# Attention with a relative bias and a gated MLP on one core: block transposes on VectorE, an eight-tile value product, and f16 operand pairs

## The chip, the cores and the metric

The kernel runs on one core of a Trainium2 chip. The core has a matmul engine (PE, whose weight loads the profile lists apart as PEld), three engines for everything else (VectorE or DVE, ScalarE or ACT, GpSimd or POOL), and SyncE (SP), whose queue issues most of the DMAs. Each engine works through its own instructions in order and waits on semaphores for the others. Matmul results land in PSUM, eight banks of 2 KB per partition; everything else is in SBUF. POOL is given no work on PSUM here. The metric is the device time of one execution in microseconds.

## The reference

Eight batches of eight heads, 576 positions, head size 64. The attention has a bias that a small two-layer network computes from the relative position, the same for all batches. Its output, with the heads side by side, is the input x of the gated MLP: a causal convolution of five taps per channel, a sigmoid of it as the gate, and two 512 x 512 products.

```python
scores = scale * np.matmul(q, k.transpose(0, 1, 3, 2))
x = (psi_rel / psi_i)[..., None]
h = np.maximum(x @ w1 + b1, 0.0)
bias = h @ w2
scores = scores + bias.transpose(2, 0, 1)[None, :, :, :]
scores = scores - np.max(scores, axis=-1, keepdims=True)
attn = np.exp(scores)
attn = attn / (np.sum(attn, axis=-1, keepdims=True) + 1e-09)
return np.matmul(attn, v).astype(np.float32)
...
for k in range(K):
    gate_pre += conv_w[k][None, None, :] * xp[:, k:k + S, :]
gate = 1.0 / (1.0 + np.exp(-gate_pre))
val = x @ w_val
return (gate * val @ w_out).astype(np.float32)
```

q, k, v and the bias network are f32; the convolution's weights and the two MLP matrices arrive as f64, which the kernel reads as pairs of 32-bit words and turns into a high and a low f32 part.

## The kernel before

**Planning.** The program does not issue its instructions in the order in which the code stands. `add` (line 87) records a task: the engines that may run it with a cost on each, the tasks it depends on, a priority, and the ring slots it takes and uses. `order` (line 100) then plays a greedy schedule through with these costs, and the tasks are emitted in its order. `OFFS` (line 56) shifts the priority of each kind of task, `LOAD` (line 55) weighs its cost when an engine is picked, `BUFS` (line 44) gives the slots of each ring, `LOOK` how far ahead of priority a task may take one, `PAIR_AT` and `MLP_AT` place each pair and each batch's MLP on the axis of priorities.

**Bias.** `bias_rows` (line 317) runs once for each 16 rows of positions: four relu passes on ACT, DVE or POOL (lines 338 and 340), matmuls with the second layer on four column tiles (line 359), an added constant on ACT or DVE (line 378), and a store of the skewed rows to DRAM. `load_bias` reads a chunk of 128 rows for a pair of heads back into SBUF when a run of pairs begins.

**Pairs.** `order` of line 275 lists 32 pairs of heads: `RUNS` (line 39) goes through the heads in two groups of four (two pairs, l = 0 and 1), in four runs; within a run the bias tiles stay. `pair` (line 526) has five chunks of query rows, four of 128 and one that holds the last 64 of both heads. For each: `qkm` multiplies Q and K in f32 on two row tiles, one head each (line 617, and line 629 for the last chunk); `logits` (line 659) adds the bias on DVE and takes the row extreme; `expo` (line 671) is the exponential on ACT with the row sum.

The attention weights must then be turned, keys onto partitions, and there are two ways, picked by `TRANS` (line 43). In 13 pairs POOL or DVE normalises (`norm`, line 716), PE transposes 128 x 128 blocks with the identity (line 756), and ACT or DVE copies them out of PSUM (`tev`). In the other 19 the exponentials are split into a high and a low f16 part (`top`, line 247 on ACT, and `rest`, line 254 on POOL), both are turned by a transposing DMA (`swap`, line 790), V is scaled and split in the same way (lines 559 to 586), and the division by the row sum comes after the value product: the reciprocals are transposed and spread over the partitions on PE (`rtp`, `rb`, lines 876 and 883) and multiplied in on DVE (`mu`, line 887). The value product itself (`piece`, line 826, and `rem_mm`, line 902) works on two column tiles of 64, one per head.

A pair of the batch's first run writes its x to DRAM (`store`), one of the second run puts it directly into the tile `xp`; the other half is read back (`ldx`).

**MLP.** `mlp` (line 943) runs for a batch when its four pairs are done. The convolution works on half rows of 288 in PSUM, on DVE (`taps`, line 1016); only the last batch uses `conv`, `prod` and `acc` on whole rows (lines 966 to 981). `val` (line 1073) and `outp` (line 1130) multiply high and low parts, three products for each, in the 32-bit single-pass format F32R; `split_hi`, `split_lo`, `ghi` and `glo` (lines 247 to 254) make those parts, `gf` (line 1083) multiplies the gate in, `ote` copies the result out of PSUM.

**PSUM.** The ring `sp` has two slots of two banks for QK, the ring `ps` four single banks for everything else.

## Time and profile before

| | |
|---|---|
| median of 3 runs | 762.93 us (762.93 to 766.36) |
| span of the profiled execution, first to last instruction | 759.0 us |
| granted clock of PE, mean | 0.995 |
| logits passes on DVE (line 659) | 256 of 750 ns and 32 of 820 ns |
| exponentials on ACT (line 671) | 256 of 774 ns and 32 of 826 ns |
| QK matmuls (line 617) | 1024 instructions of 64 rows x 128 columns, 288 moved |
| value product (line 826) | 1140 instructions in f16, 520 in f32 |
| HBM read and written | 61.03 and 25.05 MB |
| DMA packets | 263754, of which 231538 under 512 B |

An f32 matmul is two instructions in the list, an f16 or F32R one is one. "Busy" of a group is the time in which at least one of its instructions ran. Instructions of one engine overlap a little, so groups sum to more than the engine's busy time. The profiled execution ran 3.9 us shorter by its span than the median, which has what lies before the first and after the last instruction.

### The profile page before, as it was taken

To read this page: it belongs to the slowest core of one execution; us is meant where nothing else is said; L and a number is where in the kernel's file an instruction comes from. 1 tells how busy PE (TensorE), PEld (TensorE's weight loads), DVE (VectorE), ACT (ScalarE), POOL (GpSimd) and SP (SyncE) were. 2 spreads that over 40 slices of the span, in tenths; PEclk is the share of its full clock that TensorE was granted. 3 is DMA by queue.
4 is the path that set the end of the run, shared out by engine and by line. 5 is a ranking of instruction groups with operands and counts; after the bars stand their busy time and mean duration, and the time that the engine had idled before them with its cause. 6 is when DMAs were issued, how large, how long until landed. Compare 5 with 4: busy or idle time off the path is not lost.

```text
span 759.0 us, 17283 instructions
## 1 busy us (share of the span) xinstructions
PE 716.5 (94%) x6091; PEld 485.7 (64%) x6091; DVE 587.5 (77%) x1606; ACT 580.8 (77%) x1302; POOL 476.1 (63%) x550
## 2 busy tenths in 40 slices
PE   5577999999999999999899999999999999999997
PEld 2124666665566666767566677666767786767886
DVE  6996878777789897886759778869998878856830
ACT  6996788767578897889767876789797967797642
POOL 0002467765455685777975494859797587768852
PEclk9999999999999999999999999999999999999999
DMA  8898442968332878899999599599999999999702
GB/s 293 284 287 287 134 119 69 223 198 260 127 111 82 165 157 200 175 196 186 221 207 197 162 243 274 119 221 214 212 175 222 218 265 243 255 193 187 134 29 70
DMA packets 263754, 144.48 MB, mean 190 GB/s; under 512 B 231538, under 2 KB 231796, under 8 KB 263668
## 3 DMA queue, kind: packets, MB, share of 16 engines
q1 hardware_dynamic: 258420, 133.95, 76.7%
q10 hardware_dynamic: 5248, 9.44, 3.9%
q8 instruction: 48, 0.79, 0.4%
q14 instruction: 38, 0.31, 0.1%
HBM read 61.03 MB, written 25.05 MB: 113 GB/s over the span
## 4 chain that ended last, share of the span: by engine, by line
PE 50%; POOL 3%; DMA 3%; DVE 3%; ACT 2%; issue 1%; SPq 0%; POOLq 0%; DVEq 0%; ACTq 0%
PE t_ps L1073 12%; PE t_ps L1130 11%; PE t_sp L617 10%; PE t_ps L826 9%; DMA t_pt<-t_d 3%; PE t_sp L629 2%; PE t_ps L883 2%; PE t_ps L756 2%; POOL t_d L254 2%; PE t_ps L902 2%; PE t_ps L876 1%; DVE t_d L659 1%; ACT t_d L671 1%; DVE xl L254 0%; POOL xl L254 0%
## 5 line engine op out<-in xcount | busy, mean ns | idle before, releaser
L671 ACT ACTIVATE t_d<-t_d,nm 128x576 f32<-128x576 f32 x256 | 197.9, 774 | 67.7 <-DVE nm L659 67.0
L254 POOL TENSOR_TENSOR t_d<-t_d 128x576 f16<-128x576 f32 x152 | 198.1, 1315 | 36.1 <-ACT t_d L247 29.5
L659 DVE CUSTOM_DVE_ANT_0 t_d<-t_sp,bias 128x576 f32<-128x576 f32 x256 | 187.7, 750 | 35.6 <-PE t_sp L617 24.7
L716 POOL TENSOR_SCALAR t_d<-t_d,rinv 128x576 f32<-128x576 f32 x104 | 79.6, 777 | 148.5 <-DVE rinv L698 91.7
L617 PE MATMUL t_sp<-t_qk 64*128 64x288 f32 x1024 | 169.3, 432 | 3.2 <-DVE nm L659 3.1
L826 PE MATMUL t_ps<-t_pt,t_w 128*64 128x256 f16 (+1 forms) x1660 | 140.9, 311 | 4.8 <-DMA t_pt<-t_d 2.5
L617 PEld LDWEIGHTS t_sp<-t_qk 64*128 64x128 f32 x1024 | 95.0, 188 | 52.9 <-issue 13.4
L1016 DVE SCALAR_TENSOR_TENSOR t_ps<-t_xp,convw,t_ps 128x288 f32<-128x288 f32 x168 | 87.2, 519 | 5.6 <-ACT t_ps L1007 2.7
L1073 PE MATMUL t_ps<-xh,wv 128*128 128x320 f32 (+1 forms) x512 | 84.4, 302 | 1.1 <-DVE rt L249 1.1
L1073 PEld LDWEIGHTS t_ps<-xh,wv 128*128 128x128 f32 x512 | 71.9, 188 | 12.4 <-issue 7.3
L247 ACT CAST t_d<-t_d 128x576 f16<-128x576 f32 x113 | 74.6, 668 | 2.9 <-PE t_ps L756 0.4
L1130 PE MATMUL t_ps<-wo,gh 128*128 128x512 f32 x256 | 71.9, 409 | 0.7 <-ACT gh L247 0.6
L826 PEld LDWEIGHTS <-t_w 128*64 128x64 f16 x1140 | 57.4, 109 | 22.2 <-issue 18.9
L756 PE MATMUL t_ps<-identr,t_d 128*128 128x128 f32 x468 | 67.1, 281 | 0.8 <-POOL t_d L716 0.3
L756 PEld LDWEIGHTS t_ps<-identr,t_d 128*128 128x128 f32 x468 | 50.8, 140 | 23.0 <-issue 9.8
L247 ACT COPY t_pt<-t_ps 128x512 f32<-128x512 f32 (+1 forms) x104 | 50.8, 514 | 13.8 <-PE t_ps L756 13.7
L1130 PEld LDWEIGHTS t_ps<-wo,gh 128*128 128x128 f32 x256 | 44.7, 188 | 18.3 <-issue 6.4
L247 ACT COPY t_w<-t_ps 128x512 f32<-128x512 f32 (+2 forms) x65 | 32.6, 501 | 31.2 <-PE t_ps L1130 20.2
L1083 DVE TENSOR_TENSOR t_w<-t_ps,t_w 128x256 f32<-128x256 f32 (+1 forms) x64 | 29.0, 454 | 33.0 <-PE t_ps L1073 26.6
L254 POOL TENSOR_TENSOR gl<-t_w,gh 128x256 fp32r<-128x256 f32 x53 | 40.8, 771 | 16.2 <-PE t_ps L1130 12.8
L826 PEld LDWEIGHTS t_ps<-t_pt,t_w 128*64 128x64 f32 x520 | 33.0, 136 | 28.0 <-issue 10.7
L251 POOL TENSOR_SCALAR t_d<-t_d 128x576 f16<-128x576 f32 x36 | 25.2, 700 | 37.9 <-ACT t_d L671 30.4
(116 smaller groups left out, 1207.4 us busy)
## 6 DMA issues: line engine op xcount, KB each, us to landing
t_qk<-qkd SPq DMA_DIRECT2D x32, 608.0 KB, 4.7
bias<-bias_d SPq DMA_DIRECT2D x32, 576.0 KB, 5.1
bias_d<-t_be SPq DMA_DIRECT2D x36, 295.5 KB, 4.7
out<-t_w ACTq DMA_DIRECT2D x32, 256.0 KB, 3.2
t_w<-vd SPq DMA_DIRECT2D x19, 320.0 KB, 3.5
xs<-t_w SPq DMA_DIRECT2D x16, 288.0 KB, 3.6
t_xp<-xs SPq DMA_DIRECT2D x8, 576.0 KB, 4.7
t_w<-vn SPq DMA_DIRECT2D x13, 320.0 KB, 5.1
```

What stands on the lines that cost most here:

```text
L247: A.copy(out=out, in_=in_)
L254: (V if e == "V" else G).tensor_tensor(out=out, in0=in0, in1=in1, op=ALU.subtract)
L617: T.matmul(ts[a][:, j, 0:hw], lhsT=q_[r, c * P : (c + 1) * P], rhs=k_[r, a * REM + j * hw : a * REM + (j + 1) * hw], start=True, stop=True,)
L659: V.tensor_tensor_reduce(out=part().rearrange("p (j f) -> p j f", j=2), in0=sp.t[:, :, 0 : w // 2], in1=bias.rearrange("p (j f) -> p j f", ...
L671: A.activation(out=part(), in_=part(), func=AF.Exp, bias=nms[c][:, a : a + 1], scale=-1.0, accum_out=sums[c][:, a, 0:1],)
L716: (G if e == "G" else V).tensor_scalar(out=t, in0=t, scalar1=rinvs[c][:, a : a + 1], scalar2=1.0, op0=ALU.mult, op1=ALU.mult,)
L756: T.transpose(t[:, k * P : (k + 1) * P], es[c].t[:, (k0 + k) * P : (k0 + k + 1) * P], ident)
L826: T.matmul(po.t[r, 0:256], lhsT=vt.t[:, v0 + t, r], rhs=pt[:, w, :, :] if tr else pt[:, :, w, :], start=(k == 0), stop=(k == 5 * len(prods ...
L1016: V.scalar_tensor_tensor(out=o, in0=x, scalar=cw, in1=t, op0=ALU.mult, op1=ALU.add)
L1073: T.matmul(pm.t[:, 0:w], lhsT=pools["wv"][wi][:, k, d * P : (d + 1) * P], rhs=xb.t[xi][:, k, 0:w], start=(q == 0 and k == 0), stop=(q == 2 ...
L1083: V.tensor_tensor(out=gf_.t[:, 0:w], in0=pm.t[:, 0:w], in1=gates[d].t[:, t0 : t0 + w], op=ALU.mult)
L1130: T.matmul(pm.t, lhsT=gb.t[gi][:, k, o : o + P] if o < 256 else gx.t[gi][:, k, :], rhs=pools["wo"][wi][:, k, :], start=(q == 0 and k == 0) ...
```

## The change

- The runs become nine short ones, `(0, (0,)), (1, (0, 1)), (0, (1, 2)), ...`: a batch's second half follows its first at once. The spill of x to DRAM is gone; each pair's x goes directly into `xp`. The bias tiles are loaded anew for each run.
- Both ways of turning the weights are replaced by one. POOL normalises every row (`norm`, POOL alone), DVE transposes blocks of 32 x 32 in f32 (`turn_`), and the value product runs in f32 on eight tiles at a time, 32 rows x 64 columns each: V is loaded four times over the partitions for it. PE transposes, transposing DMAs, the splits of weights and V, and the rescaling afterwards are gone.
- The last 64 queries of l = 0 and l = 1 are multiplied together on four tiles of 64 x 64 (`qkr`).
- The MLP's operands become pairs of f16 values. For this x, the weights and the result are scaled by powers of two that come from maxima: of V per batch (`scales`: a read of V, a reduction on DVE, a matmul with ones), of the weights once (`wm_red`, `wm_fin`). The scaling sits in the evictions (`ev`, `ote`), in `gf` and in the convolution's weights (`vm_cw`).
- The convolution of every batch is that of the last batch before, with the first of four channel blocks on DVE alone, and the sums of the other three on POOL alone.
- The ring `sp` has three slots instead of two and also holds the value product's output; `ps` has two banks instead of four. `OFFS`, `LOAD`, `LOOK`, `PAIR_AT` and `MLP_AT` have new numbers, and some costs in the tasks too; the planner's cost of a change of matmul mode is now given by mode.

```diff
-RUNS = ((0, (0, 1, 2, 3)), (1, (0, 4, 1, 5, 2, 6, 3)), (0, (4, 5, 6, 7)), (1, (7,)))
+RUNS = ((0, (0,)), (1, (0, 1)), (0, (1, 2)), (1, (2, 3)), (0, (3, 4)), (1, (4, 5)), (0, (5, 6)), (1, (6, 7)), (0, (7,)))
...
-BUFS = dict(w=13, d=5, pt=2, sp=2, ps=4, qk=3, rel=4, be=6, xp=2, xh=1, gh=1, gx=1, rt=2)
+BUFS = dict(w=10, d=5, pt=2, vx=2, sp=3, ps=2, qk=2, rel=3, be=6, xp=2, xh=1, gh=1, gx=1)
...
-DRAIN = 0.07
+DRAIN = (0.18, 0.21, 0.16, 0.16, 0.16)
...
-LOAD = dict(P=0.95, V=1.2, A=0.36, G=0.47, S=0.08)
+LOAD = dict(P=0.87, V=0.69, A=0.25, G=0.68, S=1.63)
...
+        def vm_red(e):
+            t = vb.t.rearrange("p j d -> p (j d)")
+            V.tensor_reduce(out=osc[b][:, 1:2], in_=t, op=ALU.max, axis=AX.X, apply_absolute_value=True)
...
+        nr = [add([("G", 0.73)], partial(norm, a=a), [t], h + heads + 0.6 + a / 2) for a in range(heads)]
...
+                def qkr(e, sps=sps):
+                    ts = [new(sp, [P, 2, 512], F32) for sp in sps]
+                    for j in range(2):
+                        for y, q_ in enumerate((qk, qk2)):
+                            for a, r in enumerate((top_, bot)):
+                                x = (j + a) % 2
+                                T.matmul(
+                                    ts[y][(top_, bot)[(a + y) % 2], x, 0:HS],
+                                    lhsT=q_.t[r, NM * P : S],
+                                    rhs=q_.t[r, S + x * HS : S + (x + 1) * HS],
+                                    start=True,
+                                    stop=True,
+                                )
...
+            def turn_(e, c=c, eb=eb, first=first):
+                if first is None:
+                    new(xt, [P, 2 * NM + 1, S], F32)
+                if c < NM:
+                    V.transpose(out=xt.t[:, c : 9 - c : 8 - 2 * c, :], in_=eb.t.rearrange("p (a f) -> p a f", a=2))
                 else:
+                    V.transpose(out=xt.t[:, NM, :], in_=eb.t)
...
+        avs = [Buf("sp") for _ in range(2)]
+
+        def av(e, j0):
+            if j0 == 0:
+                for sp in avs:
+                    new(sp, [P, 2, 512], F32)
+            pv = xt.t.rearrange("p s (j q) -> p s j q", q=32)
+            for j in range(j0, j0 + NJ // 3):
+                for i in range(4):
+                    for a in range(2):
+                        k = NM + (i // 2 == (a + l) % 2)
+                        r, o = slice(32 * i, 32 * i + 32), (top_, bot)[a]
+                        T.matmul(
+                            avs[i // 2].t[o, i % 2, 0 : 32 * k],
+                            lhsT=vx.t[r, j, o],
+                            rhs=pv[r, 0:k, j, :] if a == 0 else pv[r, 8 : 8 - k : -1, j, :],
+                            start=j == 0,
+                            stop=j == NJ - 1,
                         )
...
+            t = add([("A", 0.58), ("V", 0.5)], partial(ev, h=h), d, s0 + 13.5, [xo] if new_ else (), [avs[h]])
...
-                elif k >= 2:
-                    y = add([("A", 0.67), ("G", 0.75)], prod, d[:1], x - 0.2, [tmp], [xp])
-                    convs[k] = add([("V", 0.67), ("G", 1.3)], acc, [convs[k], y], x, (), [tmp])
+                elif k >= 1:
+                    y = add([("A", 0.67), ("G", 0.75)], prod, d[:2], x - 0.2, [tmp], [xp])
+                    convs[k] = add([("G", 1.45)], acc, [convs[k], y], x, (), [tmp])
                 else:
                     convs[k] = add([("V", 0.73)], conv, d, x, (), [xp])
...
-                        xb.t = [pools["mp"].tile([P, NK, 320], F32R, name=x, tag=x) for x in ("xh", "xl")]
+                        xb.t = [pools["mp"].tile([P, NK, 320], F16, name=x, tag=x) for x in ("xh", "xl")]
```

## The prediction

> **What bounds the kernel now.** I read the page's busy times first, then the busy time by stretch, the chain that ended last, and the groups by line.

> ```profile
> span 759.0 us, 17283 instructions
> PE 716.5 (94%) x6091; PEld 485.7 (64%) x6091; DVE 587.5 (77%) x1606; ACT 580.8 (77%) x1302; POOL 476.1 (63%) x550
> ...
> PE 50%; POOL 3%; DMA 3%; DVE 3%; ACT 2%; issue 1%; SPq 0%; POOLq 0%; DVEq 0%; ACTq 0%
> ```
> ```profile
> 0.00:80.00 80.00, 54.47 (x486) 22.75 (x487) 64.32 (x171) 62.82 (x135) 8.83 (x34) 0.96 0.84 278
> 80.00:720.00 640.00, 628.12 (x5396) 434.56 (x5393) 515.36 (x1421) 505.60 (x1141) 451.86 (x497) 1.00 0.85 188
> 720.00:759.10 39.10, 33.95 (x213) 28.39 (x212) 7.86 (x15) 12.37 (x27) 15.40 (x21) 0.99 0.14 48
> ```

> The columns of the second fence are the stretch, then PE, PEld, DVE, ACT, POOL busy, the granted clock, DMA share and GB/s. From 80 to 720 us, where the pairs run, PE is busy 628.1 of 640 us at full clock: it loses 1.9% and sets the pace. DVE and ACT stand idle a fifth of that stretch. The first 80 us (the bias rows) are not PE's: all three engines are below 81% there, and the pairs need those rows. The last 39 us are PE's again, the last batch's MLP, with DVE idle 31 of them. So the question is what PE still has to do, and which engine takes its place.

> **What PE loses.** The matmul groups, then pieces of the chain (start, length, line, instructions), which show a group's length from its start to the next group's:

> ```profile
> L617 PE MATMUL t_sp<-t_qk 64*128 64x288 f32 x1024 | 169.3, 432 | 3.2 <-DVE nm L659 3.1
> L826 PE MATMUL t_ps<-t_pt,t_w 128*64 128x256 f16 (+1 forms) x1660 | 140.9, 311 | 4.8 <-DMA t_pt<-t_d 2.5 <-ACT t_pt L247 1.7 <-ACT xh L247 0.6
> L756 PE MATMUL t_ps<-identr,t_d 128*128 128x128 f32 x468 | 67.1, 281 | 0.8 <-POOL t_d L716 0.3 <-ACT t_pt L247 0.2
> L629 PE MATMUL t_sp<-t_qk 64*64 64x320 f32 x256 | 41.4, 442 | 4.7 <-DVE nm L659 4.6
> L883 PE MATMUL t_ps<-rt,sel 2*128 2x256 f32 x76 | 26.4, 426 | 0.3 <-ACT t_w L855 0.3
> L902 PE MATMUL t_ps<-t_w 128*64 128x64 f16 (+1 forms) x830 | 23.0, 207 | 0.0
> L876 PE MATMUL t_ps<-identr,rinvs 128*2 128x128 f32 x76 | 14.3, 271 | 0.0
> L756 PE MATMUL t_ps<-identr,t_w 128*128 128x128 f32 x65 | 10.0, 279 | 0.7 <-POOL t_w L716 0.3 <-ACT t_pt L247 0.2
> L912 PE MATMUL t_ps<-identr,rinvs 128*64 128x64 f32 x76 | 5.9, 236 | 0.0
> ```
> ```profile
> 290.09 1.17 PE t_sp L617 x8
> ...
> 293.89 1.76 PE t_ps L826 x30
> ```
> ```profile
> 306.20 2.31 PE t_ps L826 x20
> ```
> ```profile
> 726.29 5.66 PE t_ps L1073 x48
> ```

> Value product, PE transposes and row rescaling (L826, L756 twice, L883, L902, L876, L912) make 287.6 us. The 17 PE groups of that view (nine stand here) sum to 785 where the page has 716.5, since neighbours overlap, so I scale by 0.91: 262 us go. What comes is, per pair, 18 steps of eight tiles, each an f32 product of two instructions, half of them 160 columns wide. L826's 20 f32 instructions are ten pairs on two column tiles in 2.31 us: 0.231 us for 256 columns, so 0.144 for 160. If all eight tiles run side by side the wider ones set the step: 18 x 2 x 0.144 = 5.2 us, and 0.2 for a group's start (L617: 1.17 us, of which four pairs of 288 columns at 256-column speed less its start, 0.24 each, are 0.96). 32 x 5.4 = 173 us. The trace has two row tiles side by side (L617) and two column tiles (L826), never four rows: bounds 4.3 us (18 steps of the mean 144 columns without any start) and 10.4 (four tiles at a time). I take 5.4, nearest to rows in which every tile shown does run beside its neighbour.

> The last queries, 41.4 us for 32 groups, become 16 groups of four tiles, 1.3 us each: 21, so 20 go. The MLP's f16 pairs: 30 f16 instructions of 256 columns on two column tiles take 1.76 us, 0.117 a pair; 48 single-pass f32 ones take 5.66, 0.118 each. Between nothing and the 8% that a group's start may hide, 0 to 16 us; I take 10. PE: 716.5 - 262 + 173 - 20 - 10 = **598 us**. It stops being the bound.

> **What DVE takes on.**

> ```profile
> L659 DVE CUSTOM_DVE_ANT_0 t_d<-t_sp,bias 128x576 f32<-128x576 f32 x256 | 187.7, 750 | 35.6 <-PE t_sp L617 24.7 <-DMA bias<-bias_d 3.8 <-POOL t_d L254 3.4
> L1016 DVE SCALAR_TENSOR_TENSOR t_ps<-t_xp,convw,t_ps 128x288 f32<-128x288 f32 x168 | 87.2, 519 | 5.6 <-ACT t_ps L1007 2.7
> L1016 DVE SCALAR_TENSOR_TENSOR t_w<-t_xp,convw,t_ps 128x288 f32<-128x288 f32 x56 | 28.8, 515 | 2.3
> L575 DVE SCALAR_TENSOR_TENSOR t_w<-t_w,vsc 128x640 f16<-128x640 f32 x19 | 20.7, 1090 | 0.5 <-ACT t_w L572 0.5
> L559 DVE TENSOR_REDUCE vsc<-t_w 128x1 f32<-128x640 f32 x19 | 15.4, 810 | 2.5 <-DMA t_w<-vd 2.5
> L249 DVE COPY t_pt<-t_ps 128x512 f32<-128x512 f32 x22 | 15.0, 682 | 0.2
> L966 DVE SCALAR_TENSOR_TENSOR t_w<-t_xp,convw,t_w 128x576 f32<-128x576 f32 x8 | 11.3, 1444 | 1.7 <-ACT t_w L970 1.7
> L887 DVE TENSOR_TENSOR t_xp<-t_xp,t_ps 128x256 f32<-128x256 f32 x24 | 10.0, 418 | 4.8 <-ACT t_xp L855 4.7
> L340 DVE TENSOR_SCALAR rel<-gt,sct,nb 128x576 f32<-128x576 f32 x6 | 3.1, 569 | 0.0
> ```
> ```profile
> 405.07 0.74 DVE L659 CUSTOM_DVE_ANT_0 t_d<-t_sp,bias 128x576 f32<-128x576 f32 x1
> 405.74 0.08 DVE L659 DVE_READ_ACCUMULATOR2_ANT nm<- 128x1 f32 x1
> 405.74 0.22 DVE L923 TENSOR_TENSOR t_xp<-t_xp,t_ps 128x64 f32<-128x64 f32 x1
> ```

> The timeline shows 0.67 us from one 0.74 us logits pass to the next instruction: packed, an instruction costs its length less 0.07, and 576 elements cost 0.60 + 0.07. A block transpose is on no row. Per pair there are four of 1,152 elements and one of 576. At the logits' 1.04 ns an element they cost 1.27 and 0.67 us, 5.75 a pair, **184 us** in all. Below stands the L340 speed (569 ns for 576, so 0.86 ns an element: 1.0 us), above the contended L966 (1444 ns: 2.9 us). I take the first, from passes that, like it, read one SBUF stream. [...]

> Removed: the convolution on half rows (L1016, 116.0), the value splits (L575, 20.7; L559, 15.4), the copies out of PSUM (L249, 15.0 and smaller), the rescaling (L887 and smaller), L966 (11.3): about 210 us, some 185 packed. Added besides the transposes: the first block's four taps, 576 wide with two SBUF inputs, which is L966's form: 32 x 1.44 = 46 (half of it if POOL were not in the way); the per-batch maximum over 2,304 elements (2.5 us by L559's speed) and the weights' maxima, 34 with their small steps; 38 more sums and reciprocals of the softmax, 6. Net 587.5 - 185 + 184 + 46 + 34 + 6 = 673. That base holds about 35 us which a full queue saves (some 500 of 1606 instructions that ran with nothing behind them, 0.07 each), and the greedy plan can send a few splits elsewhere: about **630 us**, bounds 605 and 670.

> **ACT and POOL.**

> ```profile
> L671 ACT ACTIVATE t_d<-t_d,nm 128x576 f32<-128x576 f32 x256 | 197.9, 774 | 67.7 <-DVE nm L659 67.0
> L254 POOL TENSOR_TENSOR t_d<-t_d 128x576 f16<-128x576 f32 x152 | 198.1, 1315 | 36.1 <-ACT t_d L247 29.5
> L716 POOL TENSOR_SCALAR t_d<-t_d,rinv 128x576 f32<-128x576 f32 x104 | 79.6, 777 | 148.5 <-DVE rinv L698 91.7
> L247 ACT CAST t_d<-t_d 128x576 f16<-128x576 f32 x113 | 74.6, 668 | 2.9 <-PE t_ps L756 0.4
> L981 POOL TENSOR_TENSOR t_w<-t_w 128x576 f32<-128x576 f32 x8 | 12.3, 1541 | 1.4 <-ACT t_w L976 0.9
> L247 ACT COPY t_pt<-t_ps 128x512 f32<-128x512 f32 (+1 forms) x104 | 50.8, 514 | 13.8 <-PE t_ps L756 13.7
> ```

> ACT drops casts and copies (74.6 + 50.8 and smaller) and takes products and evictions of about the same sum: it stays below 580. POOL drops the subtractions (198.1), and gets all 288 normalisations (0.777: 224) and 96 accumulations (1.541: 148): about 510. Neither binds; both are links between DVE's logits and its transposes. New waits: a transpose stands in DVE's queue until POOL has normalised both heads, and behind it stand the next logits, for which ACT waits; that is in the 3% below. The added loads I cost at nothing. By their shapes, 40 more main bias tiles of 0.59 MB, V four times over (1.18 MB a pair) and the maxima's reads are some 65 MB; at the 278 GB/s of the first 80 us that is 234 us of some 650, while 114 transposing DMAs and the spill of x go. The loads run under the previous pair's softmax; if that cover is gone, a late bias tile stops SP and the V and QK loads queued behind it, 5 us or so at each of eight changes of run.

> **The sum**, on the span of 759.0. DVE's 630; its idle in the first 80 us, 16 (80 - 64.3); its idle beside the last MLP, 28 (31 now); and between them 3% of some 560 us, 18, against the 1.9% that PE loses now, since DVE's work hangs on three engines. 630 + 16 + 28 + 18 = 692. The median, 762.9, lies 3.9 above the span, so **696 us**.

> **Rivals.**
> - *DVE packed like PE today, or less work* (splits elsewhere, taps uncontended): 605 to 615 + 44 + 6: 655 to 670.
> - *The PSUM ring is the clock.* There are three two-bank slots; a QK group takes two, and the value product's outputs hold two. Per pair, 4.5 times (1.17 + a 0.67 logits pass + 0.3 of hand-overs) is 9.6, and 5.4 of product with 1.5 of eviction and hand-over 6.9: 16.5 us at least, with no QK in those 6.9. DVE needs (692 - 80 - 39)/31 = 18.5 a pair. The 24.7 us for which logits wait on L617 speak for it, at two slots. So 0.45 us of queueing per group makes it equal to DVE; with 0.65 it is 19.4 a pair: 80 + 31 x 19.4 + 39 + 4 = 724; with 0.9, 20.5 and 759.
> - *Row tiles overlap poorly.* [...] Worked from rows: L617's 0.96 of 1.17 is 0.82; the product becomes 6.5 us, PE 633, and if half of the added 35 us falls where DVE waits for it, 714.
> - *Slower: the transpose takes two cycles an element*, 2.5 us. DVE rises by 128 x 1.2 + 32 x 0.6 = 173, to a time of 870. It turns from faster to slower at 1.27 + 67/144 = 1.74 us, since 144 full ones share the 67 us gained. L340 and L659 speak against it, L966's 2.9 for it.
> - *The eight tiles run four at a time*, 10.4 us: PE 758, time about 800, slower too.
> - *No gain:* the work removed from PE was all hidden. PE's 98% in the middle speaks against it.

> **Chances.** Forecast (672 to 725) 0.48; better packed 0.16; ring above 725, 0.16; poor row overlap 0.08; slower by transpose 0.06, by tiles 0.03; no gain 0.03. Eight in ten lie between 650 and 752: below it little of the packed case, above it the slower ones and the worst of the ring. Faster by over 0.5% (about what a measurement can tell here) 0.88, within 0.5% 0.03, slower 0.09.

> **What would show it.** Right: DVE busy above 88%, transposes near 1.3 us, the product in three groups of about 1.8 us, PE near 600 and below 90%, a chain split over engines. Wrong: transposes over 1.74 us; product groups over 2.2; logits waiting for L617's successor over 60 us in all with DVE below 85% (the ring); a granted clock under 0.98.

## The result: slower by 5.8%, and the profile after

The changed kernel takes 808.88 us (median of 4 runs, 806.53 to 813.1) where the kernel before takes 763.04: a ratio of 1.058, 95% interval 1.053 to 1.063. The forecast was 696, with 650 to 752 as its range, so the sign was wrong too. The first lines of the page of the changed kernel, its instruction queue, and its chain by engine:

```profile
span 804.7 us, 28607 instructions
...
PE 670.2 (83%) x12072; PEld 421.2 (52%) x12072; DVE 643.0 (80%) x1562; ACT 523.5 (65%) x1141; POOL 462.5 (57%) x548
...
q8 instruction: 95, 1.56, 0.8%
...
PE 26%; DVE 7%; issue 4%; POOL 1%; ACT 1%; DMA 1%; POOLq 0%; ACTq 0%; DVEq 0%
```

DVE, ACT and POOL are near or below what was forecast (630, below 580, about 510). PE fell by 46 us, not 118. Nothing is full: 83% is the largest share. Two things are new. PE has 12,072 matmuls and as many weight loads, twice as many as before (6,091 of each). And in the chain "issue", time in which an engine waits for nothing that the profile shows, went from 1% to 4%.

The groups of instructions by line give the place. The columns are those of before: line, engine, operation, tiles, shape, count, busy time, mean ns, and the idle time before them with what ended it.

```profile
L752 PE MATMUL t_sp<-t_qk 64*128 64x288 f32 x1024 | 203.0, 465 | 37.8 <-DVE nm L686 36.7 <-ACT xp L251 0.8
L811 PE MATMUL t_sp<-t_pt,t_vx 32*64 32x160 f32 (+1 forms) x9216 | 197.8, 308 | 60.7 <-issue 56.2 <-DVE nm L686 2.2 <-DVE xp L253 2.2
...
L772 PE MATMUL t_sp<-t_qk 64*64 64x288 f32 x256 | 22.9, 451 | 1.2 <-DVE nm L686 1.2
```
```profile
L686 DVE CUSTOM_DVE_ANT_0 t_d<-t_sp,bias 128x576 f32<-128x576 f32 x256 | 187.5, 739 | 23.8 <-PE t_sp L752 23.4
L790 DVE STREAM_TRANSPOSE t_pt<-t_d 128x1152 f32<-128x1152 f32 x128 | 173.3, 1362 | 29.4 <-PE t_sp L811 24.8 <-POOL t_d L712 4.3
...
L792 DVE STREAM_TRANSPOSE t_pt<-t_w 128x576 f32<-128x576 f32 x32 | 24.4, 763 | 0.6 <-POOL t_w L712 0.6
L626 DVE TENSOR_REDUCE osc<-t_vx 128x1 f32<-128x2304 f32 x8 | 20.3, 2539 | 1.4 <-DMA t_vx<-vf 1.4
```

L811 is the value product, and 56.2 us of "issue" stand before its instructions. The transposes cost what was forecast (1.36 us each and 0.76), but wait 24.8 us for the product. One product in the timeline (start, length, line, instructions, and in brackets the idle time before):

```profile
299.32 2.93 PE L811 MATMUL t_sp<-t_pt,t_vx 32*64 32x160 f32 x148
...
302.74 2.16 PEld L811 LDWEIGHTS t_sp<-t_pt,t_vx 32*64 32x64 f32 x128 [0.79 <-issue]
302.75 2.44 PE L811 MATMUL t_sp<-t_pt,t_vx 32*64 32x160 f32 x128 [0.50 <-issue]
306.75 0.22 PEld L811 LDWEIGHTS t_sp<-t_pt,t_vx 32*64 32x64 f32 x12 [1.84 <-issue]
306.75 0.52 PE L811 MATMUL t_sp<-t_pt,t_vx 32*64 32x160 f32 x12 [1.57 <-issue]
...
307.28 1.03 ACT L251 ACTIVATE xp<-t_sp,xsc 128x256 f32<-128x256 f32 x3 [6.49 <-PE t_sp L811]
...
307.45 1.38 DVE L790 STREAM_TRANSPOSE t_pt<-t_d 128x1152 f32<-128x1152 f32 x1 [6.84 <-PE t_sp L811]
```

The product breaks off twice, after 148 matmuls and after 128 more, and waits for nothing that is named. Between the two breaks lie 128 matmuls and 128 loads: 256 instructions. It is so in the whole trace. Inside products, 46 pauses are longer than 0.4 us, 71 us in all. If PE's instructions are numbered in the order of their starts, its semaphore instructions among them, 39 of these pauses (64 us) end with an instruction whose number leaves one and the same remainder when divided by 256; the other seven make 6 us. Queue q8, which carries instructions, moved 1.56 MB in 95 packets, 16 KB each, and 24,144 matmuls and loads are 94.3 times 256: one packet for each 256 of them. In the trace's DMA records the next packet starts 1.15 us (the median) after such a number is passed, and at 85 of the 95 such numbers not before: at these it is fetched once the packet before it is begun. The packets that the 39 pauses wait for take 0.9 to 1.4 us, and each pause ends 1.2 to 1.6 us after its packet has landed. Together that is some 3.5 us for 256 instructions. While PE pauses, ACT cannot empty the product's banks (6.49 us) and DVE cannot write the next transposed tile, since there are two of them (6.84 us).

The stretches show what is left. Columns: PE, PEld, DVE, ACT and POOL busy, the granted clock, DMA share, GB/s.

```profile
0.00:80.00 80.00, 55.50 (x398) 18.77 (x398) 64.21 (x177) 66.86 (x128) 10.74 (x29) 0.98 0.92 314
80.00:160.00 80.00, 52.86 (x998) 34.43 (x998) 67.31 (x158) 39.90 (x91) 42.72 (x44) 0.79 0.54 170
160.00:240.00 80.00, 63.36 (x1180) 43.52 (x1186) 74.40 (x171) 55.94 (x116) 60.82 (x58) 0.74 0.55 188
...
740.00:810.00 70.00, 56.77 (x856) 35.63 (x848) 37.39 (x92) 31.76 (x71) 23.34 (x25) 0.98 0.10 36
```

By the forecast's own sum: DVE works 643 us (forecast 630); it is idle 15.8 us in the first 80 (forecast 16) and 27.3 after 740 (64.7 - 37.4; forecast 28). What is left, 804.7 - 643.0 - 15.8 - 27.3 = 118.6 us, is its idle time in between, where the forecast had 18. Of the 113 us of the miss 101 lie there, and 13 in DVE's own work.

### The profile page after: what moved, and what is told of

Read it like the earlier page. It is cut to its first block, busy times and chain, and to the rows that moved or that the text cites. A ratio compares the mean times of both kernels' runs of the same rounds, so it can differ in the third digit from the quotient of the medians.

```text
span 804.7 us, 28607 instructions
## 1 busy us (share of the span) xinstructions
PE 670.2 (83%) x12072; PEld 421.2 (52%) x12072; DVE 643.0 (80%) x1562; ACT 523.5 (65%) x1141; POOL 462.5 (57%) x548
## 3 DMA queue, kind: packets, MB, share of 16 engines
q8 instruction: 95, 1.56, 0.8%
## 5 line engine op out<-in xcount | busy, mean ns | idle before, releaser
L712 POOL TENSOR_SCALAR t_d<-t_d,rinv 128x576 f32<-128x576 f32 x256 | 201.2, 799 | 128.1 <-DVE rinv L708 112.0
L811 PE MATMUL t_sp<-t_pt,t_vx 32*64 32x160 f32 (+1 forms) x9216 | 197.8, 308 | 60.7 <-issue 56.2
L752 PE MATMUL t_sp<-t_qk 64*128 64x288 f32 x1024 | 203.0, 465 | 37.8 <-DVE nm L686 36.7
L811 PEld LDWEIGHTS t_sp<-t_pt,t_vx 32*64 32x64 f32 x9216 | 173.3, 138 | 86.8 <-issue 75.5
L686 DVE CUSTOM_DVE_ANT_0 t_d<-t_sp,bias 128x576 f32<-128x576 f32 x256 | 187.5, 739 | 23.8 <-PE t_sp L752 23.4
L790 DVE STREAM_TRANSPOSE t_pt<-t_d 128x1152 f32<-128x1152 f32 x128 | 173.3, 1362 | 29.4 <-PE t_sp L811 24.8
L884 POOL TENSOR_TENSOR t_w<-t_w 128x576 f32<-128x576 f32 x96 | 137.2, 1430 | 22.3 <-ACT t_w L879 18.8
L944 PEld LDWEIGHTS <-wv 128*128 128x128 f16 x768 | 71.6, 100 | 49.1 <-issue 30.0
L944 PE MATMUL t_ps<-xh,wv 128*128 128x320 f16 (+1 forms) x512 | 80.1, 295 | 5.6 <-DVE t_w L954 3.7
L1006 PE MATMUL t_ps<-wo,gh 128*128 128x512 f16 x256 | 64.4, 384 | 1.0 <-ACT gh L243 0.4
L350 PE MATMUL t_sp<-rel,w 128*32 128x288 f32 (+17 forms) x352 | 48.0, 511 | 18.3 <-ACT rel L328 6.6
L879 ACT ACTIVATE t_w<-xp,convb 128x576 f32<-128x576 f32 x76 | 55.9, 763 | 4.4 <-DVE rinv L708 2.4
L350 PEld LDWEIGHTS t_sp<-rel,w 128*32 128x32 f32 x352 | 14.4, 116 | 50.8 <-ACT rel L328 18.5
```

The lines of the kernel that those rows point to most:

```text
L350: T.matmul(pb.t[32 * g : 32 * g + 32, j, 0 : y - x], lhsT=w28, rhs=rel[g].t[:, x:y], start=True, stop=True, tile_position=(0, 32 * g),)
L686: V.tensor_tensor_reduce(out=eb.t[:, a * S : (a + 1) * S].rearrange("p (j f) -> p j f", j=2), in0=sps[a].t[:, :, 0:HS], in1=bias.rearrange ...
L712: (G if e == "G" else V).tensor_scalar(out=t, in0=t, scalar1=st["r"][:, a : a + 1], scalar2=1.0, op0=ALU.mult, op1=ALU.mult)
L752: T.matmul(ts[a][:, j, 0:HS], lhsT=qk.t[r, c * P : (c + 1) * P], rhs=qk.t[r, S + j * HS : S + (j + 1) * HS], start=True, stop=True,)
L790: V.transpose(out=xt.t[:, c : 9 - c : 8 - 2 * c, :], in_=eb.t.rearrange("p (a f) -> p a f", a=2))
L811: T.matmul(avs[i // 2].t[o, i % 2, 0 : 32 * k], lhsT=vx.t[r, j, o], rhs=pv[r, 0:k, j, :] if a == 0 else pv[r, 8 : 8 - k : -1, j, :], start ...
```

## The experiments

Theory 1: PE's instructions arrive in packets of 256, one takes about 3.5 us from the start of the packet before it to its own use, and a product of 576 instructions (288 matmuls, 288 loads) waits for them. Theory 2: the tiles overlap worse than thought, so columns set its length. Theory 3: the order of work or the other engines set the time, and PE's pauses are cover.

**Fewer columns, same instructions** (after the first of the 18 steps a matmul moves 32 columns; most of the product is left out).

```diff
-                        k = NM + (i // 2 == (a + l) % 2)
+                        k = NM + (i // 2 == (a + l) % 2) if j == 0 else 1
```

> The changed kernel, but from the second of the 18 steps of the value product on, each matmul moves 32 columns instead of 128 or 160; it leaves out most of the product and issues as many instructions as before. Theory 1 (PE waits for its instructions: 256 of them per fetch, one fetch about every 3.5 us, so 576 instructions take 7.9 us whatever they compute): a product stays at 7 to 8 us and the time at 790 to 815 us. Theory 2 (the eight tiles stream too slowly): a product falls to 2 to 3 us and the time by 80 us or more. Theory 3 (three PSUM slots are the clock): as theory 2, since the product's slots come free sooner.

Measured: 811.81 us (one run), inside the changed kernel's scatter. The product's row of the groups:

```profile
L811 PE MATMUL t_sp<-t_pt,t_vx 32*64 32x32 f32 (+2 forms) x9216 | 135.5, 254 | 92.8 <-issue 85.7 <-DVE nm L686 4.6 <-DVE xp L253 2.4
```

About a quarter of the columns, and the time does not fall. Of the 62 us of busy time that go (197.8 to 135.5), 30 come back as issue (56.2 to 85.7). By the starts of its matmuls a product still takes 7.05 us on the mean, where theory 2 gave 2 to 3: theory 2 falls. The 27 us that the 32 products do save are lost elsewhere: at a granted clock of 0.825 (0.933 in the changed kernel) the MLP's matmuls alone take 23 us more (208.5 to 231.9).

**More instructions, hardly more columns** (a matmul of one column more for each row tile from the second step on, 848 instructions per product with the loads; it adds one column of the product a second time).

```diff
+                        if a == 0 and j:
+                            T.matmul(
+                                avs[i // 2].t[o, i % 2, 0:1],
+                                lhsT=vx.t[r, j, o],
+                                rhs=pv[r, 0, j, 0:1],
+                                start=False,
+                                stop=False,
+                            )
```

> The changed kernel with one more matmul of a single column for each row tile from the second step on, 848 PE instructions per product instead of 576; it adds one column of the product a second time. Theory 1: 848/256 x 3.5 = 11.6 us per product instead of 7.9, and 90 to 120 us more in all. Theory 2: a column costs next to nothing beside 128 to 160, so at most 20 us more.

Measured: 931.47 us (one run), 122.6 more than the changed kernel: as theory 1 had it and slightly more: 3.8 us for each of 32 products, 14.1 ns for each of 272 added instructions, which is 3.6 us for 256. Theory 3 falls: an instruction that moves one column costs the whole program its share of a packet.

**Half the instructions, three times the columns** (the upper halves of both operands, read as bfloat16, need one pass and not two: 4,608 matmuls in the list for 9,216; the columns are moved three times. The lower 16 bits of the product's operands are left out).

```diff
+            BF = mybir.dt.bfloat16
+            pv = xt.t.bitcast(BF).rearrange("p s (j q t) -> p s j q t", q=32, t=2)[:, :, :, :, 1]
+            vv = vx.t.bitcast(BF).rearrange("p j (d t) -> p j d t", t=2)[:, :, :, 1]
...
-                            avs[i // 2].t[o, i % 2, 0 : 32 * k],
-                            lhsT=vx.t[r, j, o],
+                            avs[i // 2].t[o, i % 2, 0 : 96 * k],
+                            lhsT=vv[r, j, o],
```

> The changed kernel with the value product in one pass on the upper halves of the f32 words (bfloat16), and each matmul moving its columns three times over; this leaves out the lower bits of both operands. 288 PE instructions per product instead of 576, at 384 to 480 columns of one pass each, some 0.2 us a step against 0.27 before. Theory 1: a product takes 4.0 to 4.6 us, and the time falls by 70 to 100 us, to 705 to 740, which is about where the prediction put a kernel whose product streams undisturbed. Theory 2: a product takes three quarters of 7.9, 6 us, and the time falls by 50 us at most.

Measured: 735.49 us (4 runs), ratio to the kernel before 0.962, 0.956 to 0.967: faster than both. The product's row now has no issue in front:

```profile
L813 PE MATMUL t_sp<-t_pt,t_vx 32*64 32x384 bf16 (+1 forms) x4608 | 137.4, 362 | 12.7 <-DVE nm L686 4.8 <-DVE t_pt L792 3.1 <-DVE xp L253 2.8
```

**The planner told of the packets** (the routine that orders the work adds a wait of 3.5 us per 256 PE instructions to its cost of PE; the computation is the same).

```diff
+                    cross = (count + t.ins) // PAGE * PAGE
+                    if cross > count:
+                        at = max(s + cost * (cross - count) / t.ins, arrives)
+                        cost = at - s + cost * (count + t.ins - cross) / t.ins
+                        arrives = at + FETCH
+                    count += t.ins
```

> The changed kernel, the same computation, with one rule more in the planner: the 256th instruction of a page cannot start before 3.5 us after the first of the page before, and a step of the product costs 0.273 us. The order of all engines follows from it. Theory 1: the planner cannot remove the waits, it can only place other work in them, so 775 to 805 us. Theory that the waits matter little and that the order is what is wrong: 740 or less.

Measured: 811.28 us (4 runs), ratio 1.061, 1.052 to 1.071: no better than the changed kernel. This expectation missed by 6 us. 51.3 us of issue stay in front of the product there: an order cannot take instructions out of it.

**Half the instructions in f32, same columns.** The bfloat16 run changed the type as well as the count, and streams for less time (137.4 us of busy time for 197.8). Here the product keeps f32 and its two passes, takes every second block of keys (half the product is left out), and moves each column twice. The expectation's count of instructions is twice too high: it is 144 matmuls and 144 loads per pair, half of the changed kernel's 288 and 288.

```diff
-            for j in range(j0, j0 + NJ // 3):
+            for j in range(j0, j0 + NJ // 3, 2):
...
-                            avs[i // 2].t[o, i % 2, 0 : 32 * k],
+                            avs[i // 2].t[o, i % 2, 0 : 64 * k],
```

> The product stays in f32 with its order and tiles, but takes only every second block of 32 keys and moves its columns twice, so that it streams as many columns as the changed kernel with half as many instructions (288 multiplications, 576 with the weight loads, per pair). It leaves out half of the value product. Theory 1 (instruction fetch is the clock of the product): the stalls go, the product takes what its columns take, 9 steps of 2 x 0.273 us, so 4.9 to 5.3 us per pair where the changed kernel has 7.9, and the time falls to 740 to 770 us, above the 735.5 of the one-pass product by the longer product. Rival (an f32 product with its two passes is slow for a reason of its own, not for its count of instructions): 7 to 8 us per pair and 795 to 815 us. Forecast's other steps: if all of them held, the time at this product length would be 696 us; if it lands near 755, the fetch explains only about half of the miss, and the rest lies in the way DVE and PE wait for each other.

Measured: 739.62 us (4 runs, ratio 0.967, 0.961 to 0.973), at the low edge of what theory 1 gave. The product's row, and a product in its timeline:

```profile
L811 PE MATMUL t_sp<-t_pt,t_vx 32*64 32x256 f32 (+1 forms) x4608 | 180.3, 432 | 8.2 <-issue 2.8
```
```profile
289.36 5.10 PE L811 MATMUL t_sp<-t_pt,t_vx 32*64 32x320 f32 x144
294.39 1.05 PE L944 MATMUL t_ps<-xh,wv 128*128 128x256 f16 x8
```

One piece of 5.03 us from start to start, at its full number of columns. So the forecast's 5.2 us for streaming was right, and f32 is not slow for a reason of its own. The seven products that start before 235 us take 6.1 to 8.6 us, and the mean is 5.75: 184 us for all 32, where the forecast had 173 and the changed kernel 253. This run also divides the miss: with the fetch out of the way and the product near the forecast's length the time is 739.6, so the fetch is worth 69 of the 113 us, as much as the products lose by their starts, and 44 remain. DVE's idle time between head and tail falls from 118.6 to 56.6 us. The stretches:

```profile
80.00:240.00 160.00, 124.39 (x1348) 81.97 (x1355) 145.96 (x337) 99.95 (x215) 111.75 (x108) 0.73 0.56 182
240.00:400.00 160.00, 152.35 (x1728) 92.24 (x1714) 140.22 (x345) 117.11 (x265) 119.60 (x152) 0.99 0.57 190
400.00:560.00 160.00, 153.77 (x2062) 96.80 (x2060) 147.26 (x357) 115.25 (x260) 113.03 (x136) 0.99 0.62 207
560.00:640.00 80.00, 77.77 (x938) 47.87 (x937) 74.06 (x175) 59.56 (x138) 59.88 (x72) 0.98 0.60 191
```

From 80 to 240 us DVE is busy 91% and PE's clock is 0.73; from 240 to 640 PE is busy 383.9 of 400 us, 96%, and DVE 90%. By 240 us QK groups worth 8.0 pairs have run, as in the changed kernel; in the kernel before it was 11.2. The next runs ask which of these makes up the 44 us.

**A still shorter product** (one pass, columns once), and **the same with the planner's constants chosen anew** for a product piece of 1.2 us.

```diff
-                            avs[i // 2].t[o, i % 2, 0 : 96 * k],
+                            avs[i // 2].t[o, i % 2, 0 : 32 * k],
```

> The product in one pass on the upper halves (bfloat16) of both operands, each column moved once: a third of the columns of the run before with columns three times over (288 multiplications per pair, as there). It leaves out the lower 16 bits of the two operands of the value product. Theory 1: 576 instructions at 13.7 ns are 3.9 us per pair at most and its columns only about 1.3, so fetches and not columns set it: 3 to 3.9 us, and the time stays within 10 us of 735.5. Rival (columns set the product): 1.3 to 1.6 us per pair, PE has 2 us a pair more, and the time falls to 705 to 722 us.

> The same one-pass product with the planner's offsets, due times and looks chosen anew for a product piece of 1.2 us instead of 1.53; nothing else is computed or left out than in the run before. The planner's own length falls from 722.6 us with the old constants and that cost to 689.5. If order is what holds DVE and PE apart in the middle (43 us of DVE idle there in the run with columns three times over, 18 forecast), 705 to 725 us; if the planner's gains do not carry to the chip, 730 to 745.

Measured: 748.08 and 738.00 us (4 runs each). The first missed both ways. The counts of its text are twice too high as above; a product of 288 instructions crosses one or two packets' ends, and where the next packet is there already it takes 1.47 us, so the 13.7 ns per instruction holds for long bursts only (mean 2.65 us with pauses and waits). But the time rose by 12.6 us over the run with columns three times over, in the same order and with as many instructions. PE's clock is one likely reason. The early stretches of the first of the two runs:

```profile
80.00:160.00 80.00, 49.75 (x582) 29.16 (x582) 72.95 (x172) 45.96 (x101) 47.55 (x47) 0.62 0.63 203
160.00:240.00 80.00, 52.85 (x886) 33.19 (x885) 74.55 (x168) 54.60 (x115) 64.49 (x62) 0.63 0.52 170
240.00:320.00 80.00, 66.04 (x769) 37.56 (x770) 68.37 (x164) 54.89 (x124) 53.98 (x69) 0.89 0.57 191
```

PE has more pauses here (from 80 to 240 us it is busy 102.6 of 160 us, in the half-instruction run 124.4) and was granted less: 0.62 where the half-instruction run has 0.73, 0.89 where it has 0.98, and over the run 0.85 against 0.92 with columns three times. By the starts of the matmuls the products take 58 us less (143 to 85), but the QK groups 42 more (299 to 341) and the MLP 31 more (212 to 243). The clock is not alone in that: pauses at packet ends make 23 us (2 us with columns three times), half of them outside the product, and the QK groups wait 15 us longer for ACT to empty the product's banks (23.1 for 8.5). No run separates the three. The new order brought 10 us back, and its planner had promised 33.

**Columns three times in the new order.**

> The newly ordered run with the one-pass product, but with its columns moved three times as in the first one-pass run, so that PE works longer on the same result: 3.6 us a product instead of 1.5 to 2.2. It leaves out the lower 16 bits of the product's operands. The granted clock was 0.86 with columns once and 0.92 with them three times. If the clock that PE loses by its pauses is what the shorter product gave back, the granted clock rises above 0.90 and the time falls below the 738.0 of the same order, to 715 to 733. If PE's own length counts, 740 to 760.

Measured: 734.40 us (4 runs, ratio 0.962, 0.957 to 0.967), granted clock 0.918. Just above the range of the first case: 3.6 us below the same order with columns once; it cannot be told from the 735.49 of the old order. So this other order gains nothing, and raising the clock from 0.86 to 0.92 by longer products gains little.

**Less DVE work**: the maximum over V over 128 of 2,304 columns, in the half-instruction kernel and in the changed one (most of that maximum is left out).

```diff
-            V.tensor_reduce(out=osc[b][:, 1:2], in_=t, op=ALU.max, axis=AX.X, apply_absolute_value=True)
+            V.tensor_reduce(out=osc[b][:, 1:2], in_=t[:, 0:P], op=ALU.max, axis=AX.X, apply_absolute_value=True)
```

> The run with half the instructions of the product once more, and besides it the maximum over V reads 128 of its 2,304 columns (8 instructions of 2.54 us become about 0.2, so 18 to 19 us of DVE work go). It leaves out half of the value product and most of the maximum. DVE was 641 of 738 us there. If DVE is the clock once the fetch is out of the way (its 641 and what it cannot fill), 739.6 falls by 14 to 19 us, to 720 to 726. If the order and the chain from engine to engine hold it (DVE idle grows by what it sheds), it falls by less than 7, to 733 to 740.

> The changed kernel with the same shorter maximum over V and nothing else changed; it leaves out most of that maximum. If PE with its fetches is the clock from 240 us on, 18 us less on DVE give little: a gain only in the first quarter, 0 to 8 us, so 801 to 809. If DVE is the clock here too, 14 to 19 us: 790 to 795.

Measured: 734.89 us (4 runs), 4.7 less than with the maximum, and 805.16 (798.5 to 808.62), 3.7 less than the changed kernel, which its scatter hardly tells from nothing. DVE shed 15 us in the first (640.9 to 625.8) and idles for most of them. DVE alone does not set the time.

**Less DVE work where it is fullest**: of the eight blocks of MLP weights six are copies of the first of their matrix and not prepared (six blocks are left out), in the half-instruction kernel and in the one with columns three times.

```diff
+            if k == 0:
+                wdone = weight(src.bitcast(I32)[k * P : (k + 1) * P, :], DM, hi_lo, k, wdone, pri)
+                continue
+            for y in range(2):
+                def w_same(e, k=k, y=y, hi_lo=hi_lo):
+                    copy(e, pools[hi_lo][y][:, k, :], pools[hi_lo][y][:, 0, :])
```

> The run with half the instructions of the product, and of the eight blocks of MLP weights only the first of each of the two matrices is prepared from its 64-bit source; the other six are copies of it. It leaves out half of the value product and six of eight weight blocks. Some 30 us of DVE work go, all of them between about 80 and 240 us, where DVE was busy 146 of 160 us and PE 124 at a granted clock of 0.73. If the excess of DVE work in that stretch is what the forecast's sum over the whole run could not see, more pairs end before 240 us and the time falls from 739.6 by 20 to 30, to 710 to 720. If the chain through all engines sets the time wherever DVE's work lies, as for the maximum over V (18 us less work, 4.7 us less time), it falls by 4 to 12, to 728 to 736.

> The same six blocks copied, in the kernel with the one-pass product whose columns move three times (735.5 us). It leaves out the lower 16 bits of the product's operands and six of eight weight blocks. PE is lighter here by 1.2 us a pair. If DVE and PE take turns as the limit (DVE before 240 us, PE with 96% in the half-instruction run from 240 to 640 us), taking from both gives more than taking from either: 695 to 712. If the order holds the time, 724 to 733.

Measured: 730.36 and 723.96 us (4 runs each): 9.3 and 11.5 less than without that edit. The first lies in the second case expected, the second at that case's edge. DVE's work fell by 23.8 and 24.7 us (640.9 to 617.2 and 645.2 to 620.5), not by the 30 expected. Some 40 to 47% of the work taken from DVE's fullest stretch comes off the time, no more.

**PE's clock in that stretch**: the QK multiplications of the first nine pairs are issued twice, so that PE pauses less; the half-instruction kernel, and the changed one, which leaves nothing out.

```diff
-                    for j in range(2):
+                    for j in (0, 1, 0, 1) if n < 9 else (0, 1):
```

> The run with half the instructions of the product, and the QK multiplications of the first nine pairs are issued twice into the same place, in the same order, so that PE has more to do where its granted clock was 0.73 (80 to 240 us). It leaves out half of the value product. If the clock in that stretch is what makes PE late, the clock there rises above 0.9, the products there take 5.0 to 5.6 us instead of 6.1 to 8.6, and the time falls from 739.6 to 715 to 730. If DVE with 146 of 160 us is the limit of that stretch whatever PE's clock is, the clock rises and the time stays at 734 to 745. If the clock stays low, the doubled groups cost up to 1.1 us each, 36 of them, and the time rises by 10 to 25.

> The changed kernel with the same doubled QK multiplications in the first nine pairs; nothing is left out. The granted clock was 0.77 from 80 to 240 us. If the clock costs time there: 780 to 800. If DVE limits that stretch: 803 to 815. With a clock that stays low: 815 to 830.

Measured: 743.42 and 814.08 us (4 runs each), both in the case that DVE limits. The stretches of the first, and one of the half-instruction kernel with fewer weight blocks:

```profile
80.00:160.00 80.00, 61.21 (x701) 41.17 (x701) 71.94 (x168) 45.98 (x101) 45.47 (x47) 0.93 0.60 186
160.00:240.00 80.00, 62.94 (x792) 42.57 (x795) 72.13 (x169) 52.56 (x110) 61.15 (x58) 0.94 0.51 172
```
```profile
160.00:240.00 80.00, 71.40 (x970) 45.69 (x970) 63.31 (x151) 52.81 (x117) 54.43 (x61) 0.94 0.51 177
```

The clock rises from 0.73 to 0.93, DVE stays at 90%, and the time does not fall. The added multiplications themselves cost PE 19 us, though (QK groups by their starts, 243 to 261), so what the same clock would give for nothing is not shown. The last line fits a low clock that follows from PE's waiting for DVE: with 10 us less DVE work there than the half-instruction kernel has (73.6 to 63.3), the clock is 0.94 without any added matmul.

## Why the prediction was wrong

**What failed: "32 x 5.4 = 173 us", the product's term in "What PE loses".** The forecast had it, with bounds 4.3 and 10.4 for one product, from columns and a group's start alone; the fetch of instructions stood in it at nothing. The columns do take 5.03 us, as the half-instruction run shows. The product takes 7.9 on the mean (252.6 us for 32, from the starts of its matmuls to what follows), because 576 instructions come as 2.25 packets of 256, each about 3.5 us. The 7.9 lies inside the bounds, but those were bounds on how tiles overlap, and no rival had a term that counts instructions. The count could have been seen: the forecast's own "18 steps of eight tiles, each an f32 product of two instructions" is 288 matmuls, each with a load. The kernel before never met it, since its 30 matmuls of L826 in 1.76 us are 60 instructions at 29 ns, twice as slow as the packets come (3.5 us for 256, 13.7 ns each).

**"It stops being the bound" failed with it.** The stretch from 240 to 720 us of the changed kernel, and the first of PE's waits in it (who waited for whom, us in total, times, the longest):

```profile
240.00:720.00 480.00, 422.10 (x8275) 275.69 (x8266) 383.96 (x932) 310.93 (x699) 311.14 (x380) 0.97 0.54 180
```
```profile
PE t_sp L811 <- issue: 40.7, 29, 3.4
PE t_sp L752 <- DVE nm L686: 9.5, 15, 1.2
```

PE has 670 us of busy time in all, not 598. By rows, 25 us of that are the product (197.8 for 173) and 34 the QK groups (203.0, which the forecast left at 169.3): between 80 and 240 us, at a granted clock of 0.77, they take 0.28 us of PE for each instruction (63.3 us for 224), and in the kernel before, at 1.00, 0.17 (51.7 for 311). The forecast had a mark for the clock and no term. PE's pauses are not cover: here it is busy 422.1 us and in "issue" for 40.7 more of the 480, so 96% are taken. The slots of the product then stay held, and DVE, which was to become the bound, waits for them.

**"Between them 3%" failed too,** and in part for another reason. The idle time of DVE between head and tail is 118.6 us, not 18. Fetches account for most (56.6 are left with half the instructions); but in the half-instruction run, where the product has its forecast length, the time is still 739.6, not 696. The forecast added DVE's work over the whole run, while the limit changes along it: from 80 to 240 us DVE is at 91% and eight pairs get done, and after that PE, with 24 pairs and nearly all MLP work before it, is at 96%. A sum over one engine sees neither. Taking 15 us from DVE anywhere, 24 from its fullest stretch, or 1.2 us a pair from PE gave 4.7, 9.3 and 4.1 us; the two last together gave 15.7. That fits two engines that limit in turn. It is not shown that this is all of the 44 us: the forecast's 696 was reached in no run, and what sets the 724 of the lightest is open.

**What was right.** Transposes 1.36 and 0.76 us each by their groups; forecast were 1.34 and 0.74, of which 0.07 overlap with the next. The second half of the longer one costs 0.60 us for 576 elements, 1.04 ns each, the speed that the prediction took from the logits passes. DVE 643 us for 630 (605 to 670), in part by luck: the first block's taps took 29.3 us for 46 (0.92 us each; in the kernel before, three of L966's eight took 0.82 to 0.89 and the four that ran mostly beside POOL's L981 1.58 to 1.99), so the other terms together were some 30 too low. The maximum over V 2.54 us for 2.5. The joint last queries 18.5 us less (41.4 to 22.9) for 20; the MLP 16 us less by the starts of its matmuls (224.8 to 208.5) for 10, at the edge of its bounds 0 to 16. ACT and POOL do not bind. Head and tail 15.8 and 27.3 us for 16 and 28.

**The rivals.** The slower side of the forecast was the transpose at 2.5 us (it takes 1.36) and tiles four at a time, 10.4 us a product (its columns take 5.03); the slower time came by neither. The PSUM ring would have shown over 60 us of logits waiting for QK; it was 23.4, and PE waited 36.7 for DVE, 27.0 of them before 240 us. Poor row overlap would make the product 6.5 us without pauses; it is 5.03. Of the marks set beforehand, product groups over 2.2 us (2.6 on the mean, 7.9 by three) and a granted clock below 0.98 (0.933) were met. By the runs with doubled QK multiplications the second looks like a symptom and not a cause.

## What to carry to other kernels

Price a burst of small matmuls twice, by its columns and by its instructions, loads and passes included: here 256 instructions cost about 3.5 us in products of 576 (one of 288 took 1.47 us where its next packet was there already), and the larger price was the nearer: 7.9 us for 576 instructions whose columns take 5.03, 5.75 us for 288 with the same columns. Halving the count at the same streaming time took 69 us off where fewer columns took nothing. And where the work is spread unevenly, sum the bound by stretch and not by engine over the whole run.
